# Routed attention and mixer on one core: where a pair's small TensorE products stand, and which PSUM buffers they use

## The chip, the cores and the metric

The kernel runs on one core of one Trainium2 chip. A core has several engines that work at the same time and wait for each other by semaphores: TensorE (PE in the profile) multiplies matrices and writes into PSUM, VectorE (DVE) and ScalarE (ACT) read PSUM and SBUF, GpSimd (POOL) works in SBUF, and DMA queues move data to and from the device memory. The metric is the device time of one execution in microseconds (us). Before the change it is 914.13 us, the median of three runs that lie between 913.77 and 915.92.

## The reference

Attention comes first: 4 batches, 8 heads, 768 positions, 64 channels a head. Every query and every key is assigned to the nearest of 16 cluster centres of its head, and a query sees only the keys of its own cluster. The result is joined over the heads and goes through a mixer over positions and then over channels.

```python
q_assign = argmax(einsum('bhsd,hcd->bhsc', q_n, c_n), axis=-1)     # normalised q, k, centroids
k_assign = argmax(einsum('bhsd,hcd->bhsc', k_n, c_n), axis=-1)
mask = q_assign[:, :, :, None] == k_assign[:, :, None, :]
scores = where(mask, q @ k.T / sqrt(D), -1e9)
attn = exp(scores - scores.max(-1)); attn = attn / (attn.sum(-1) + 1e-9)
x = (attn @ v) with heads joined                                    # (4, 768, 512)
h = relu(x.T @ w_tok1) @ w_tok2;  u = x + h.T                       # 768 -> 256 -> 768
out = u + relu(u @ w_ch1) @ w_ch2                                   # 512 -> 1536 -> 512
```

## The kernel before

The attention works on pairs of heads: 4 batches times 4 pairs are 16 pairs. A pair takes 4 steps (GROUPS), which are two halves of the queries (384 each) times two groups of three key chunks (NG = 3, 128 keys each). Scores are held with keys on the partitions, so that the sums over keys are made in two stages: adds on VectorE over the chunks, and a product with ones on TensorE over the partitions.

The mask is a product too. The one-hot cluster of each key, times 2^33 and less 2^33, multiplied with the one-hot cluster of each query gives 0 where the clusters agree and -2^33 elsewhere. It opens the accumulation in PSUM, and the f32 scores are added onto it.

The PSUM buffers while the attention runs: one of one bank for small products (`ps_w`), one for the sum over values (`ps_av`), and three of two banks for scores (`ps_sc`).

```python
    ps_w = pool("ps_w", 1, space=PSUM)
    ps_av = pool("ps_av", 1, space=PSUM)
    ps_sc = pool("ps_sc", NG, ps_sc_stack, space=PSUM)
    ...
    work = pool("work", 7, attention)           # the exponentials of one chunk each
```

One step's scores, sums and values:

```python
    def scores(m):
        ...
        scs = [ps_sc.tile([P, 2, 512], F32, tag="sc", name="sc") for _ in range(NG)]
        for src, start in ((st["ohT"], True), (st["T"], False)):      # masks, then q and k
            for i in range(NG):
                for h in range(2):
                    rows = slice(h * D, (h + 1) * D)
                    nc.tensor.matmul(
                        scs[i][:, h, 0:HS], lhsT=src[rows, 1, j0 + i], rhs=src[rows, 0, js],
                        start=start, stop=not start,
                    )
        for i in range(NG):
            ex = work.tile([P, 2, HS], F32, name="ex")
            nc.scalar.activation(out=ex, in_=scs[i][:, :, 0:HS], func=ACT.Exp, scale=SM_SCALE)

    def add_up(m):      # VectorE: the exponentials of the group are added into "sum"
    def values(m):      # TensorE: av += v.T @ ex; after the half's last group ScalarE copies av to avT
```

The small products of a pair:

```python
    def wtile(g, shape, dt, name):          # ps_sc for the first pair, ps_w for the others
    def turn(g):                            # VectorE: q and k of the next pair turned into "qkT"
    def route_products(g):
        pr = wtile(g, [P, a1 - a0, NJ, QP], F32, "pr")        # 4 matmuls, qkT with centroids
    def route(g):                           # VectorE: sim <- pr turned, mx = max, oh = (sim >= mx)
    def route_turn(g, a):                   # a = 1 keys, a = 0 queries
        po = wtile(g, [P, NJ, P], BF16, "po")
        for j in range(NJ):
            nc.tensor.transpose(out=po[:, j], in_=oh[:, a, j], identity=identb)
        if a == 0:
            # first pair: nc.vector.tensor_copy, the others:
            nc.scalar.copy(out=st["ohT"][:, 0], in_=po)
        else:
            nc.scalar.activation(out=st["ohT"][:, 1], in_=po, func=ACT.Copy, scale=BIG, bias=-BIG, ...)

    def half_sums(hi):                      # 4 matmuls: den = ones.T @ sum, of one half
        den = st["den"] = ps_w.tile([P, 2 * HJ, QP], F32, tag="w", name="den")
    def half_reciprocals(hi):               # VectorE: dent <- den turned, rcps = 1 / dent
    def half_turn(hi):                      # 3 transposes: px <- avT
        px = st["px"] = ps_w.tile([P, HJ, P], F32, tag="w", name="px")
    def half_out(hi):                       # VectorE: x = px * rcps
```

And the loop that gives the order, which is kept on each engine (m is the step over all pairs, s the step within a pair, g the pair):

```python
    for m in range(last + 3):
        g, s = divmod(m, GROUPS)
        more = g < NPAIR - 1
        if half_at(m - 3) is not None:
            half_out(half_at(m - 3))
        if more and s == 0:
            turn(g + 1)
        if more and s == 1:
            route(g + 1)
        if 1 <= m <= last:
            add_up(m - 1)
        if m < last:
            scores(m)
        ...
        if half_at(m - 2) is not None:                  # for s == 1 and s == 3
            half_sums(half_at(m - 2))
            half_reciprocals(half_at(m - 2))
        if more and s == 2:
            route_turn(g + 1, 1)
        if 1 <= m <= last:
            values(m - 1)
        if half_at(m - 2) is not None:
            half_turn(half_at(m - 2))
        if more and s == 0:
            route_products(g + 1)
        if more and s == 2:
            route_turn(g + 1, 0)
        ...     # loads; on every third step one piece of the mixer's weights is prepared,
                # by ScalarE (wh, wup), VectorE (wh, wh, wT) and GpSimd (wc)
```

After the loop comes the mixer (`ph`, `pu`, and then the channel part), which the change leaves as it is.

Of the kernel before, what the change touches and what calls it, by code (L numbers as in the profile page):

```python
# [18 lines left out]
P = 128  # L19
# [14 lines left out]
NG = 3  # L34
# [13 lines left out]
def kernel(  # L48
# [35 lines left out]
    def pool(name, bufs, stack=None, **kw):  # L84
        return (stack or fast).enter_context(
            tc.tile_pool(name=name, bufs=bufs, reuse_waits="tile", **kw)
        )
# [13 lines left out]
    loads = pool("loads", 3, attention)  # L101
    small = pool("small", 2, attention)
    qktp = pool("qktp", 2, attention)
    work = pool("work", 7, attention)
    sums = pool("sums", 2, attention)

    routing = fast.enter_context(ExitStack())
    qkpool = pool("qkpool", 2, routing, side="right")
    rsmall = pool("rsmall", 2, routing, side="right")
    pools = {}  # L110


# [3 lines left out]
    cnT = const.tile([P, H * C], F32, name="cnT")  # L116
    cnd = const.tile([P, NF, 2, C], F32, name="cnd")
    ohs = [rsmall.tile([P, 2, NJ, P], BF16, name=f"oh{i}", bufs=1) for i in range(2)]
    rcps = const.tile([P, 2 * NPAIR, 2, HJ], F32, name="rcps")
    cells = const.tile([P, NPAIR], F32, name="cells")  # L120

    W = {
# [55 lines left out]
    def weight_steps(pool, W, names):  # L178
# [6 lines left out]


        def tmp(name, dt, n):
            return pool.tile([P, WMAX], dt, tag=name, name=name)[:, 0:n]

        def load_bits(src, p):  # L190
            n = p["n"] = src.shape[1]
# [96 lines left out]
                in_=st["qk"][:, a].rearrange("p j i d -> p (j i d)"),  # L288
            )

    def wtile(g, shape, dt, name):

        if g == 0:
            return ps_sc.tile(shape, dt, tag="sc", name=name)
        return ps_w.tile(shape, dt, tag="w", name=name)

    def route_products(g, a0=0, a1=2):

        st, f = state[g], g % NF
        pr = wtile(g, [P, a1 - a0, NJ, QP], F32, "pr")  # L300
        for i in range(NQ):
            rows = slice(i * QP, (i + 1) * QP)
            nc.tensor.matmul(  # L303
                pr[rows], lhsT=cnd[:, f].rearrange("p i c -> p (i c)"),
                rhs=st["T"][:, a0:a1, :, rows].rearrange("p a j r -> p (a j) r"),
                start=True, stop=True,
            )
        st["pr"] = pr

    def route(g, a0=0, a1=2):  # L310

        st = state[g]
        NR = (a1 - a0) * NJ * 2
        sc = rsmall.tile([P, NR, C], F32, name="sim")
        nc.vector.transpose(
            out=sc.rearrange("p n c -> p (n c)"), in_=st.pop("pr").rearrange("p a j r -> p (a j r)")
        )
        mx = rsmall.tile([P, NR], F32, name="mx")  # L320
        nc.vector.reduce_max(out=mx, in_=sc, axis=AX.X)
        oh = ohs[g % 2][:, a0:a1].rearrange("p a j (h x) -> p (a j) h x", h=2)[:, :, :, 0:C]
        nc.vector.tensor_tensor(
            out=oh, in0=sc.rearrange("p (n h) c -> p n h c", h=2),
            in1=mx.rearrange("p (n h) -> p n h", h=2).unsqueeze(3).to_broadcast([P, NR // 2, 2, C]),
            op=ALU.is_ge,
        )

    def route_turn(g, a):

        st, oh = state[g], ohs[g % 2]
        if a == 1:
            st["ohT"] = qktp.tile([P, 2, NJ, P], BF16, name="ohT")
        po = wtile(g, [P, NJ, P], BF16, "po")
        for j in range(NJ):  # L340
            nc.tensor.transpose(out=po[:, j], in_=oh[:, a, j], identity=identb)  # L341
        if a == 0:
            if g == 0:
                nc.vector.tensor_copy(out=st["ohT"][:, 0], in_=po)  # L344
            else:
                nc.scalar.copy(out=st["ohT"][:, 0], in_=po)
        else:
            nc.scalar.activation(
                out=st["ohT"][:, 1], in_=po, func=ACT.Copy, scale=BIG, bias=-BIG,
                accum_out=cells[:, g : g + 1],  # L350
            )
# [7 lines left out]
    def scores(m):  # L359
        g, qh, j0 = split(m)  # L360
        st = state[g]
        js = slice(HJ * qh, HJ * qh + HJ)
        scs = [ps_sc.tile([P, 2, 512], F32, tag="sc", name="sc") for _ in range(NG)]
        for src, start in ((st["ohT"], True), (st["T"], False)):
            for i in range(NG):
                for h in range(2):
                    rows = slice(h * D, (h + 1) * D)
                    nc.tensor.matmul(  # L368
                        scs[i][:, h, 0:HS], lhsT=src[rows, 1, j0 + i], rhs=src[rows, 0, js],
                        start=start, stop=not start,  # L370
                    )
        for i in range(NG):
            ex = work.tile([P, 2, HS], F32, name="ex")
            nc.scalar.activation(out=ex, in_=scs[i][:, :, 0:HS], func=ACT.Exp, scale=SM_SCALE)  # L374
            st["ex", qh, j0 + i] = ex

    def add_up(m):
        g, qh, j0 = split(m)
        st = state[g]
        e = [st["ex", qh, j0 + i] for i in range(NG)]  # L380
        if j0 == 0:
            acc = st["sum", qh] = sums.tile([P, 2, HS], F32, name="sum")
            nc.vector.tensor_tensor(out=acc, in0=e[0], in1=e[1], op=ALU.add)
            e = e[2:]
        acc = st["sum", qh]
        for ex in e:
            nc.vector.tensor_tensor(out=acc, in0=acc, in1=ex, op=ALU.add)  # L387

    def values(m):
# [9 lines left out]
                    start=(j == 0), stop=(j == NJ - 1),  # L399
                )  # L400
        if j0 == NJ - NG:
            st["avT", qh] = sums.tile([P, HJ, P], F32, name="avT")
            nc.scalar.copy(out=st["avT", qh].rearrange("p j t -> p (j t)"), in_=st.pop("av"))

    def half_sums(hi):

        g, qh = divmod(hi, 2)
        st = state[g]
        acc = st.pop(("sum", qh)).rearrange("p h (j t) -> p (h j) t", j=HJ)
        den = st["den"] = ps_w.tile([P, 2 * HJ, QP], F32, tag="w", name="den")  # L410
        for i in range(NQ):
            rows = slice(i * QP, (i + 1) * QP)
            nc.tensor.matmul(den[rows], lhsT=ones, rhs=acc[:, :, rows], start=True, stop=True)  # L413

    def half_reciprocals(hi):
        g, qh = divmod(hi, 2)
        dt = small.tile([P, 2 * HJ, QP], F32, name="dent")
        nc.vector.transpose(
            out=dt.rearrange("p n r -> p (n r)"),
            in_=state[g].pop("den").rearrange("p n r -> p (n r)"),  # L420
        )
        nc.vector.reciprocal(
            out=rcps[:, hi].rearrange("p h j -> p (h j)"), in_=dt[:, :, 0]
        )

    def half_turn(hi):
        g, qh = divmod(hi, 2)
        st = state[g]
        avT = st.pop(("avT", qh))
        px = st["px"] = ps_w.tile([P, HJ, P], F32, tag="w", name="px")  # L430
        for i in range(HJ):
            nc.tensor.transpose(out=px[:, i], in_=avT[:, i], identity=ident)  # L432

    def half_out(hi):

        g, qh = divmod(hi, 2)
        b, f = divmod(g, NF)
        nc.vector.tensor_tensor(  # L438
            out=xs[b][:, HJ * qh : HJ * qh + HJ, f * P : (f + 1) * P].rearrange(
                "p j (h d) -> p j h d", h=2  # L440
            ),
            in0=state[g].pop("px").rearrange("p j (h d) -> p j h d", h=2),
            in1=rcps[:, hi].rearrange("p h j -> p j h").unsqueeze(3).to_broadcast([P, HJ, 2, D]),
            op=ALU.mult,
        )
        if qh == 1:
# [224 lines left out]
    def fits():  # L671

        inside = const.tile([P, 3, 2 * NPAIR * 2 * HJ], F32, name="inside")
        good = const.tile([P, 3], F32, name="good")
        flat = rcps.rearrange("p n h j -> p (n h j)")
        for i, (limit, op) in enumerate(((LIMIT, ALU.is_le), (1.0 / LIMIT, ALU.is_ge))):
            nc.vector.tensor_scalar(
                out=inside[:, i], in0=flat, scalar1=limit, scalar2=None, op0=op
# [22 lines left out]
    def begin():  # L701
# [27 lines left out]
        route_products(0, 0, 1)  # L729
        keep_warm(2)  # L730
        route_turn(0, 1)
        route(0, 0, 1)
        keep_warm(1)
        route_turn(0, 0)

    begin()
    weights = list(weight_steps(stage, W, ("tok1", "tok2", "ch1")))
    last = NPAIR * GROUPS
    HALF = GROUPS // 2
    ends = [lambda t=t: tok1(0, t) for t in range(NT)]  # L740
    for b in range(B):
        if b + 1 < B:
            ends += [lambda b=b, t=t: tok1(b + 1, t) for t in range(NT)]
        ends += [lambda b=b, j=j: tok2(b, j) for j in range(NJ)]

    def half_at(m):

        return m // HALF if 0 <= m < last and m % HALF == HALF - 1 else None

    for m in range(last + 3):  # L750
        g, s = divmod(m, GROUPS)
        more = g < NPAIR - 1
        if half_at(m - 3) is not None:
            half_out(half_at(m - 3))
        if more and s == 0:
            turn(g + 1)
        if more and s == 1:
            route(g + 1)
        if 1 <= m <= last:
            add_up(m - 1)  # L760
        if m < last:
            scores(m)
        if m == last:
            ps_sc_stack.close()
            pools["ps_m"] = pool("ps_m", 2, space=PSUM)
        if half_at(m - 2) is not None:
            half_sums(half_at(m - 2))
            half_reciprocals(half_at(m - 2))
        if more and s == 2:
            route_turn(g + 1, 1)  # L770
        if 1 <= m <= last:
            values(m - 1)
        if half_at(m - 2) is not None:
            half_turn(half_at(m - 2))
        if more and s == 0:
            route_products(g + 1)
        if more and s == 2:
            route_turn(g + 1, 0)
        if s == 1 and g + 2 < NPAIR:
            load(g + 2)  # L780
        if m == last - GROUPS:
# [254 lines left out]
```

## Time and profile before

| | before |
|---|---|
| time, median of 3 | 914.13 us (913.77 to 915.92) |
| span of the profiled execution | 914.3 us |
| granted TensorE clock, mean | 0.994 |
| TensorE busy | 895.6 us |
| VectorE busy | 507.3 us |
| ScalarE busy | 303.5 us |
| first score product of the first pair starts | 15.78 us |
| first score product of the last pair starts | 345.07 us |

In a line of the timeline stand the start, the time from the first start to the last end, the engine, the line of the program, the operation, what it writes and reads, the shape, and how many. An f32 product has two rows in the profile for each matmul of the program, a bf16 product one. `64*128` in front of a shape tells how many rows and columns of the array the product uses. Two products that use different rows or columns of the array run beside each other, as the two heads' scores do. The ends of matmuls are modelled; so the time that a group takes is better read from its start to the next group's start. A bracket at the end of a line gives how long the engine stood idle before it, and what ended that.

### The profile page before, as it was taken

How to read it: one execution, taken by the hardware profiler on the slowest of the kernel's cores; microseconds unless marked ns; L12 is line 12 of the kernel's file. 1: busy time of each engine (PE TensorE's matmuls, PEld its weight loads, DVE VectorE, ACT ScalarE, POOL GpSimd, SP SyncE). 2: the span in 40 equal slices, each digit the busy share in tenths (PEclk: the TensorE clock that was granted, in tenths of full speed). 3: DMA queues.
4: the chain of work that ended last, by engine and by line, in shares of the span. 5: the costliest groups of instructions: out<-in, count | busy, mean ns of one | idle time of the engine just before them, and what ended most of it. 6: DMA issues, size and time to landing. Idle time of an engine off the chain costs nothing.

```text
span 914.3 us, 11630 instructions
## 1 busy us (share of the span) xinstructions
PE 895.6 (98%) x4594; PEld 533.6 (58%) x4594; DVE 507.3 (55%) x851; ACT 303.5 (33%) x515; POOL 45.0 (5%) x40
## 2 busy tenths in 40 slices
PE   7999999999999999999999899999999999999997
PEld 3444444444444444444458568677686876858676
DVE  5787787787787875577463244333443334433342
ACT  2655565565565654231130121211212012130210
POOL 1000010010010100131000000000000000000000
PEclk9999999999999999999999899999999999999999
DMA  9725426325334100240000001000010000100001
GB/s 154 157 54 107 82 70 109 80 75 99 76 85 89 62 27 1 65 143 1 0 1 1 0 1 47 23 1 1 0 47 24 0 1 12 47 12 1 1 12 61
DMA packets 112830, 41.76 MB, mean 46 GB/s; under 512 B 101632, under 2 KB 105728, under 8 KB 112768
## 3 DMA queue, kind: packets, MB, share of 16 engines
q1 hardware_dynamic: 109632, 40.55, 19.4%
q10 hardware_dynamic: 3136, 0.39, 0.4%
q8 instruction: 38, 0.62, 0.3%
q14 instruction: 24, 0.20, 0.1%
HBM read 34.64 MB, written 6.29 MB: 45 GB/s over the span
## 4 chain that ended last, share of the span: by engine, by line
PE 92%; DVE 5%; DMA 1%; issue 1%; ACT 0%; DVEq 0%
PE sc L368 16%; PE pX L652 14%; PE pX L601 14%; PE av L397 13%; PE pZ L652 7%; PE pZ L601 7%; PE ph L470 5%; PE pu L479 5%; PE pY L652 3%; PE pY L601 3%; PE px L432 2%; DVE sum L387 2%; PE po L341 2%; PE den L413 1%; PE pr L303 1%; PE pt L542 1%
## 5 line engine op out<-in xcount | busy, mean ns | idle before, releaser
L374 ACT ACTIVATE ex<-sc 128x768 f32<-128x768 f32 x192 | 141.8, 812 | 117.5 <-PE sc L368 117.5
L397 PE MATMUL av<-ex,va 128*64 128x384 f32 x768 | 138.0, 494 | 0.0
L387 DVE TENSOR_TENSOR sum<-sum,ex 128x768 f32<-128x768 f32 x128 | 130.1, 1016 | 10.1
L368 PE MATMUL sc<-qkT 64*128 64x384 f32 x768 | 134.3, 482 | 0.0
L368 PEld LDWEIGHTS sc<-qkT 64*128 64x128 f32 x768 | 71.4, 187 | 38.0
L397 PEld LDWEIGHTS av<-ex,va 128*64 128x64 f32 x768 | 49.4, 136 | 66.2 <-issue 59.8
L601 PE MATMUL pX<-uT,wc 128*128 128x384 f32 x192 | 68.8, 495 | 1.6 <-issue 1.6
L609 ACT COPY p<-pX 128x384 f32<-128x384 f32 x24 | 11.4, 475 | 153.1 <-PE pX L601 153.1
L601 PEld LDWEIGHTS pX<-uT,wc 128*128 128x128 f32 x192 | 36.7, 193 | 26.7 <-issue 3.3
L223 POOL TENSOR_TENSOR wc<-wT,wup 128x512 int32<-128x512 int32 x24 | 32.4, 1349 | 251.2 <-DVE wT L216 251.2
L368 PE MATMUL sc<-ohT 64*128 64x384 bf16 x384 | 42.6, 327 | 0.6 <-DVE ohT L344 0.6
L479 PE MATMUL pu<-h,wt 128*128 128x512 f32 x96 | 42.0, 592 | 0.0
L470 PE MATMUL ph<-x,wt 128*128 128x512 f32 x96 | 42.0, 593 | 0.0
L496 DVE TENSOR_TENSOR x<-pX,x 128x256 f32<-128x256 f32 x24 | 10.2, 424 | 55.1 <-PE pX L652 55.1
L496 DVE TENSOR_TENSOR c<-pZ,u 128x384 f32<-128x384 f32 x24 | 13.4, 557 | 46.8 <-PE pZ L601 46.8
L652 PE MATMUL pX<-w2s,hA 128*128 128x256 f32 x144 | 36.4, 390 | 0.5 <-DVE x L496 0.5
L438 DVE TENSOR_TENSOR x<-px,rcps 128x384 f32<-128x384 f32 x32 | 17.8, 556 | 33.5 <-PE px L432 33.5
L496 DVE TENSOR_TENSOR hA<-pY,p 128x384 f32<-128x384 f32 x24 | 13.4, 557 | 40.4 <-PE pY L601 40.4
L652 PE MATMUL pX<-wc,hA 128*128 128x256 f32 x144 | 35.0, 379 | 0.0
L601 PE MATMUL pZ<-uTs,w1s 128*128 128x384 f32 x96 | 35.0, 487 | 0.0
L652 PE MATMUL pX<-w2s,hS 128*128 128x256 f32 x144 | 35.0, 379 | 0.0
L652 PE MATMUL pZ<-wc,hS 128*128 128x256 f32 x144 | 35.0, 379 | 0.0
(115 smaller groups left out, 1227.0 us busy)
## 6 DMA issues: line engine op xcount, KB each, us to landing
raw<-in_moe_w_ch_dram SPq DMA_DIRECT2D x24, 512.0 KB, 3.9
qk<-in_k_dram SPq DMA_DIRECT2D x64, 96.0 KB, 4.4
va<-in_v_dram SPq DMA_DIRECT2D x16, 384.0 KB, 3.3
out_dram<-x SPq DMA_DIRECT2D x24, 256.0 KB, 2.0
qk<-in_q_dram SPq DMA_DIRECT2D x60, 96.0 KB, 3.6
raw<-in_moe_w_tok_dram SPq DMA_DIRECT2D x3, 512.0 KB, 5.8
raw<-in_moe_w_tok_dram SPq DMA_DIRECT2D x4, 384.0 KB, 4.2
qk<-in_q_dram ACTq DMA_DIRECT2D x4, 96.0 KB, 4.8
```

The source lines that it names most:

```text
L223: nc.gpsimd.tensor_tensor(out=dst.bitcast(I32), in0=T, in1=up, op=ALU.add)
L341: nc.tensor.transpose(out=po[:, j], in_=oh[:, a, j], identity=identb)
L368: nc.tensor.matmul(scs[i][:, h, 0:HS], lhsT=src[rows, 1, j0 + i], rhs=src[rows, 0, js], start=start, stop=not start,)
L374: nc.scalar.activation(out=ex, in_=scs[i][:, :, 0:HS], func=ACT.Exp, scale=SM_SCALE)
L387: nc.vector.tensor_tensor(out=acc, in0=acc, in1=ex, op=ALU.add)
L397: nc.tensor.matmul(st["av"][h * D : (h + 1) * D], lhsT=st["va"][:, h, j], rhs=ex[:, h], start=(j == 0), stop=(j == NJ - 1),)
L432: nc.tensor.transpose(out=px[:, i], in_=avT[:, i], identity=ident)
L470: nc.tensor.matmul(pf, lhsT=W["tok1"][:, j, t * P : (t + 1) * P], rhs=xs[b][:, j], start=(j == 0), stop=(j == NJ - 1),)
L479: nc.tensor.matmul(pu, lhsT=W["tok2"][:, t, j], rhs=h1s[b][:, t], start=(t == 0), stop=(t == NT - 1))
L496: nc.vector.tensor_tensor(out=dst, in0=a, in1=b, op=ALU.add)
L601: nc.tensor.matmul(psum, lhsT=A[a][:, k, c * P : (c + 1) * P], rhs=R[r][:, k], start=start and k == 0, stop=k == 1, skip_group_check=not s ...
L652: nc.tensor.matmul(psum, lhsT=h2[a][:, k, i * P : (i + 1) * P], rhs=Bw[w][:, 3 * part + k], start=start and k == 0, stop=k == 2, skip_grou ...
```

## The change

The small products of a pair move to three places. In step 1, after the values, the denominators of the pair before (both halves at once) and the routing products of the pair after are made next to each other. In step 2, after the values, all twelve cluster transposes stand next to each other, ahead of their two copies, and the output transposes of the pair before's first half follow. In step 3 those of its second half stand alone. The denominators and routing products share one of the three score buffers, each with a bank of its own, and so do the two sets of cluster transposes; `ps_w` is left to the output transposes.

As a score buffer that a small product has used comes back later, and is then the third of the next step, the masks of the third chunk are moved behind the scores of the first two. The copy of the queries' clusters goes from ScalarE to VectorE for every pair. `sum` and `avT` hold both halves of a pair; to make room, the exponentials have six buffers in place of seven, and some other temporaries one in place of two.

```diff
-    work = pool("work", 7, attention)
+    work = pool("work", 6, attention)
-    rsmall = pool("rsmall", 2, routing, side="right")
+    rsmall = pool("rsmall", 1, routing, side="right")
...
+            bufs = 1 if name == "wT" else 2
...
-        for src, start in ((st["ohT"], True), (st["T"], False)):
-            for i in range(NG):
-                for h in range(2):
+        for chunks in (range(NG - 1), (NG - 1,)):
+            for src, start in ((st["ohT"], True), (st["T"], False)):
+                for i in chunks:
+                    for h in range(2):
...
+    def route_copy(g, a):
         if a == 0:
-            if g == 0:
-                nc.vector.tensor_copy(out=st["ohT"][:, 0], in_=po)
-            else:
-                nc.scalar.copy(out=st["ohT"][:, 0], in_=po)
+            nc.vector.tensor_copy(out=st["ohT"][:, 0], in_=po)
...
+    def pair_denominators(g):
+        dt = state[g]["dt"] = small.tile([P, 4 * HJ, QP], F32, name="dent", bufs=1)
+        nc.vector.transpose(out=dt.rearrange("p n r -> p (n r)"), in_=state[g].pop("den"))
+
+    def pair_reciprocals(g):
         nc.vector.reciprocal(
+            out=rcps[:, g].rearrange("p i h j -> p (i h j)"), in_=state[g].pop("dt")[:, :, 0]
         )
...
     for m in range(last + 3):
         g, s = divmod(m, GROUPS)
         more = g < NPAIR - 1
-        if half_at(m - 3) is not None:
-            half_out(half_at(m - 3))
+        old = g - 1 if m < last else -1
+        if s == 2:
+            if old >= 0:
+                pair_denominators(old)
+            if more:
+                route(g + 1)
+            if old >= 0:
+                pair_reciprocals(old)
+        if s == 3 and old >= 0:
+            half_out(old, 0)
+        if s == 0 and old >= 1:
+            half_out(old - 1, 1)
         if more and s == 0:
             turn(g + 1)
-        if more and s == 1:
-            route(g + 1)
         if 1 <= m <= last:
             add_up(m - 1)
         if m < last:
             scores(m)
+        if 1 <= m <= last:
+            values(m - 1)
+        if m < last and s == 1:
+            two = ps_sc.tile([P, 2, 512], F32, tag="sc", name="small")
+            if old >= 0:
+                pair_sums(old, two[:, 0, 0:HS])
+            if more:
+                route_products(g + 1, pr=two[:, 1, 0:HS])
+        if m < last and s == 2:
+            if more:
+                two = ps_sc.tile([P, 2, 1024], BF16, tag="sc", name="po")
+                for a in (1, 0):
+                    po = two[:, a, 0 : NJ * P].rearrange("p (j t) -> p j t", j=NJ)
+                    route_turn(g + 1, a, po)
+                for a in (1, 0):
+                    route_copy(g + 1, a)
+            if old >= 0:
+                half_turn(old, 0, ps_w.tile([P, HS], F32, tag="w", name="px"))
+        if m < last and s == 3 and old >= 0:
+            half_turn(old, 1, ps_w.tile([P, HS], F32, tag="w", name="px"))
...     # the lines of half_sums, route_turn, values, half_turn and route_products that stood here are gone
+        if m == last + 1:
+            pair_sums(NPAIR - 1, ps_w.tile([P, HS], F32, tag="w", name="den"))
+            pair_denominators(NPAIR - 1)
+            pair_reciprocals(NPAIR - 1)
+            half_turn(NPAIR - 1, 0, ps_w.tile([P, HS], F32, tag="w", name="px"))
+            half_turn(NPAIR - 1, 1, ps_av.tile([P, HS], F32, name="av"))
```

## The prediction

> **What bounds the kernel now.** I read part 1 of the page first, then its chain, then the attention part in order of time, because the change touches only that part.
>
> ```profile
> PE 895.6 (98%) x4594; PEld 533.6 (58%) x4594; DVE 507.3 (55%) x851; ACT 303.5 (33%) x515; POOL 45.0 (5%) x40
> PE 92%; DVE 5%; DMA 1%; issue 1%; ACT 0%; DVEq 0%
> ```
>
> TensorE (PE) is busy 98% of the span, and the chain that ended last runs through it for 92%. So a microsecond counts only if TensorE does less, pauses less between products, or waits less. A share of 98% does not say that it streams all the time: the pauses are inside it. They show in the timeline of TensorE over one pair of heads (start, length, then the product):
>
> ```profile
> 206.28 0.66 PE L368 MATMUL sc<-ohT 64*128 64x384 bf16 x6
> 206.77 2.10 PE L368 MATMUL sc<-qkT 64*128 64x384 f32 x12
> 208.80 0.53 PE L413 MATMUL den<-sum,ones 128*32 128x192 f32 x8
> 209.26 2.16 PE L397 MATMUL av<-ex,va 128*64 128x384 f32 x12
> 211.35 0.55 PE L432 MATMUL px<-ident,avT 128*128 128x128 f32 x3
> 211.83 0.66 PE L368 MATMUL sc<-ohT 64*128 64x384 bf16 x6
> ...
> 216.44 0.85 PE L303 MATMUL pr<-qkT,cnd 128*32 128x384 f32 x8
> 217.23 0.66 PE L368 MATMUL sc<-ohT 64*128 64x384 bf16 x6
> ...
> 222.91 0.55 PE L432 MATMUL px<-ident,avT 128*128 128x128 f32 x3 [0.54 <-DVE dent L418]
> ...
> 225.92 0.51 PE L341 MATMUL po<-identb,oh 128*128 128x128 bf16 x6
> 226.36 2.16 PE L397 MATMUL av<-ex,va 128*64 128x384 f32 x12
> ```
>
> I take start to next start as a block's cost: scores 2.52 us (206.28 to 208.80), values 2.09 (209.26 to 211.35), denominators den 0.46, output transposes px 0.48, routing products pr 0.79, cluster transposes po 0.44. A pair has four score and four value blocks, two each of po, den and px, and one pr: 4 x 4.61 + 2 x 1.38 + 0.79 = 21.99. The table by stretches says 22.00 for undisturbed pairs and 22.61 for the pair with the wait on 222.91:
>
> ```profile
> 200.78:223.39 22.61, 22.07 (x164) 10.16 (x164) 17.48 (x25) 12.53 (x19) 2.54 (x2) 1.00 0.54 111
> 234.44:256.44 22.00, 22.00 (x163) 10.15 (x162) 17.14 (x24) 12.40 (x19) 3.01 (x2) 1.00 0.41 78
> ```
>
> (Columns: length, then busy time of PE, PEld, DVE, ACT, POOL.) DVE works 17.1 to 17.5 us of such a pair: not the bound, but the nearest to it.
>
> Now the pause. den streams two rows of 192 columns, pr two rows of 384, in the same shape of the array. If a block is a fixed toll plus its streaming s, 0.46 = toll + s and 0.79 = toll + 2s: s = 0.33, toll = 0.13. For po: a bf16 score row of 384 columns passes in 0.16 (three in 0.49), so 128 columns take 0.054, six take 0.32, and 0.12 is left over. So **every change of block costs some 0.12 us in which nothing streams**, and a pair of 22 us has 15 blocks (8 large, 7 small).
>
> The wait at 222.91: px needs the one small PSUM buffer that den holds until DVE has turned it, and DVE is late:
>
> ```profile
> 214.16 3.04 DVE L387 TENSOR_TENSOR sum<-sum,ex 128x768 f32<-128x768 f32 x3
> 217.12 0.42 DVE L206 TENSOR_SCALAR wh<-wh 128x512 f32<-128x512 f32 x1
> ...
> 218.10 0.69 DVE L216 SCALAR_TENSOR_TENSOR wT<-raw,wh 128x512 uint32<-128x512 uint32 x1
> 218.72 0.57 DVE L317 STREAM_TRANSPOSE sim<-pr 128x384 f32<-128x384 f32 x1
> ...
> 222.48 0.37 DVE L418 STREAM_TRANSPOSE dent<-den 128x192 f32<-128x192 f32 x1
> ```
>
> A weight piece (0.42 + 0.43 + 0.69, wh to wT) stands ahead of the routing and the sums, so dent starts at 222.48 although den began at 219.75. This happened in three of the pairs.
>
> **What the skill says.** (1) The Trainium skill, "TensorEngine Tiling (Array Packing)", section Key Properties: changing the tiling mode, not just the tile, drains TensorE. The trace agrees: the blocks have modes 64\*128, 128\*64, 128\*32 and 128\*128, and the toll of 0.12 to 0.13 stands at each change, while bf16 masks to f32 scores, both 64\*128, pass without one (206.28 to 206.77 is three steps of 0.16). (2) "TensorE: Matmul & The Clock Gate", section The mechanism: matmuls start and end in program order. Agrees: at 222.91 ready scores stood behind the waiting px. So a score chunk whose buffer isn't free should stand as late as it can. (3) "SBUF — State Buffer", section Who interferes with whom: a DVE instruction with two SBUF inputs contends with GpSimd reads. Agrees: one add to sum takes 958 ns in the middle and up to 1849 ns. I take up to 0.9 us of such delay per weight piece below.
>
> **The change, part by part.**
> *Gathering.* Den of both halves (2s) and pr (2s) become one 128\*32 block: 4 x 0.33 + 0.13 = 1.45, before 2 x 0.46 + 0.79 = 1.71. Twelve po and the first px become one 128\*128 block: 0.64 + 0.36 + 0.12 = 1.12, before 2 x 0.44 + 0.48 = 1.36. The second px stays, 0.48. Seven small blocks become three, so four tolls fall away (a pair has 11 blocks in place of 15). Sum 3.05 in place of 3.55: **0.50 less per pair, 21.5**. A full gathered pair exists 14 times: 7.0 us.
> *Waits taken away.* den and pr leave the single small buffer, so px waits only for the multiply of the pair before. The 14 pairs from 35.01 to 345.07 took 310.06, or 22.15 each against 22.00: 2.1 us waiting, gone.
> *First pair and tail.* The first pair has no den and px of its own any more, 0.94, and one toll less: -1.05. The last pair gets one den of 0.79 in place of 0.46 + 0.46, one of them at the tail, and px follows den through the single buffer there as before: 1.23 from den to px now, of it the relu at 0.69 and dent at 0.37. With dent twice as wide (0.58, as the sim turn) that is some 0.5 more. With the den and px handed on from the first pair: +0.65. Together -0.4.
> *Third chunk behind two.* Per step the order is masks and scores of two chunks, then masks and scores of the third: one more change f32 to bf16 and back, inside mode 64\*128. bf16 to f32 is free; f32 to bf16 occurs nowhere in this trace. I choose 0.01 us, 64 times: +0.6.
> *DVE and ACT.* The copy of ohT's query half moves from ACT (0.80) to DVE (0.56, from its single case before). One dent of 0.58 replaces two of 0.38, one reciprocal two of 0.19: DVE +0.2 net, 17.5 of 21.5. Off the path.
> Sum: -7.0 - 2.1 - 0.4 + 0.6 = -8.9, from 914.1 to **905.2, say 905**. The mixer part after the attention keeps its instructions.
>
> **Rivals.**
> *A: the score slots become the wait.* den/pr and po now take one of the three score slots, which returns as the next step's third chunk. From the last-but-one step's start, den/pr begin at 4.6 and end near 5.9; DVE turns pr from 6.1 to 6.7. The next step begins at 6.0 and needs the slot 1.6 later, at 7.6. DVE's own queue: turn and sums of step 0 end 5.6 after its start, or 7.3 with a weight piece, so 2.7 into step 1; two adds (2.0) and 0.9 of GpSimd contention reach 5.6, dent 6.2, sim 6.8. Free by 7.0: no wait, with 0.6 to spare. After po: ACT's copy (0.83 + 0.22) ends some 1.2 after po, the slot is needed 0.5 (px) + 1.6 after: 0.8 to spare. If I am wrong by 0.5 in every pair, +7: 912. Where only weight pairs slip by 0.5: 907.
> *B: the f32 to bf16 change costs a toll.* 64 x 0.1 = 6.4: 911. Against: the mode stays the same.
> *C: DVE becomes the bound.* It would need 21.5 a pair and has 17.5. Against.
> *D: six exp buffers in place of seven.* exp of a step then waits for the sums of two steps back. The worst DVE lag above, 2.7 us, still ends the first add in time; a slip of 0.2 on ACT doesn't reach TensorE. Time as predicted.
> *E: the merged blocks pay less.* If po to px has no pause at all for the f32 weights, 0.06 a pair more: 904.
>
> **Range and chances.** A alone at its mild size and B at a third give 907 to 909; E and a smaller tail 903. So 902.5 to 910. Faster by 2% needs 895.8, more than twice the tolls and waits that I can find; slower by 2% needs a wait of 1.7 us per pair. Chances 0.02, 0.96, 0.02.
>
> **What would show it.** In the changed profile: pairs of 21.5 from score start to score start; den and pr as one block of about 1.4, po with px of about 1.1; score blocks still 2.52 (2.6 or more: B); no wait of px on dent but the last; no wait of sc on dent, sim or the ohT copy (some: A); DVE about 17.5 a pair. The mixer from its first ph on should keep its length to 1 us. Wrong would be the sum if the toll were a matter of each shape and not of the change of mode: then den and pr together would keep 1.7.

## The result, and the profile after

| | before | after |
|---|---|---|
| time, median of 6 | 914.87 us (913.77 to 915.92) | 904.85 us (903.71 to 906.34) |
| span of the profiled execution | 914.3 us | 904.5 us |
| 14 pairs of heads, from the second to the fifteenth | 310.06 us | 300.63 us |

The ratio is 0.9891, with a 95% interval of 0.9876 to 0.9905: about 10 us less. The prediction was 905.0 us with a range of 902.5 to 910.

Part 1 of the page after, and its chain:

```profile
PE 887.6 (98%) x4466; PEld 530.5 (59%) x4466; DVE 506.6 (56%) x834; ACT 295.8 (33%) x500; POOL 44.7 (5%) x40
PE 97%; DMA 1%; DVE 1%; ACT 0%; issue 0%
```

TensorE's share is the same 98%, and it is still the bound. Its busy time fell by 8.0 us, because the pauses between blocks count as busy here. VectorE, which stood in the chain with 5%, is at 1%: no wait on it is left in the pairs.

The timeline of TensorE over steps 1 and 2 of a pair after the change:

```profile
213.16 2.16 PE L400 MATMUL av<-ex,va 128*64 128x384 f32 x12
215.25 0.85 PE L417 MATMUL small<-sum,ones 128*32 128x384 f32 x8
215.91 0.83 PE L299 MATMUL small<-qkT,cnd 128*32 128x384 f32 x8
216.68 0.50 PE L369 MATMUL sc<-ohT 64*128 64x384 bf16 x4
217.01 1.45 PE L369 MATMUL sc<-qkT 64*128 64x384 f32 x8
218.30 0.33 PE L369 MATMUL sc<-ohT 64*128 64x384 bf16 x2
218.46 0.81 PE L369 MATMUL sc<-qkT 64*128 64x384 f32 x4
219.20 2.16 PE L400 MATMUL av<-ex,va 128*64 128x384 f32 x12
221.29 0.84 PE L338 MATMUL po<-identb,oh 128*128 128x128 bf16 x12
221.97 0.50 PE L430 MATMUL px<-ident,avT 128*128 128x128 f32 x3
222.40 0.50 PE L369 MATMUL sc<-ohT 64*128 64x384 bf16 x4
```

Read start to start: den with pr takes 1.43 (215.25 to 216.68), po with px 1.11 (221.29 to 222.40). The score block is still 2.52 (216.68 to 219.20) although its masks are now in two places: f32 to bf16 at 218.30 comes 1.29 after 217.01, which is four rows of 0.32, without a pause. The stretches show a single pair, and then 14 pairs together (columns: length, the busy time of PE, PEld, DVE, ACT, POOL, then granted clock, DMA share and GB/s):

```profile
205.93:227.40 21.47, 21.47 (x156) 9.96 (x154) 18.40 (x26) 13.07 (x20) 1.86 (x1) 1.00 0.39 80
34.23:334.86 300.63, 300.63 (x2159) 139.38 (x2158) 238.76 (x334) 169.87 (x258) 25.45 (x19) 1.00 0.39 81
```

300.63 / 14 = 21.47: every pair takes the same time, and TensorE's busy time equals the length of the stretch. The rest of the difference is small: the first pair gained 0.75 (18.47 in place of 19.22), the stretch from the last pair's first score to the last pair's px and the next `ph` lost 0.54 (40.20 in place of 39.66). From there to the end the two kernels take 529.5 and 529.4.

### The profile page after: what moved, and what is told of

Same layout as the page of the kernel before. It is cut to its first block, busy times and chain, and to the rows that moved or that the text cites. A ratio compares the mean times of both kernels' runs of the same rounds, so it can differ in the third digit from the quotient of the medians.

```text
span 904.5 us, 11304 instructions
## 1 busy us (share of the span) xinstructions
PE 887.6 (98%) x4466; PEld 530.5 (59%) x4466; DVE 506.6 (56%) x834; ACT 295.8 (33%) x500; POOL 44.7 (5%) x40
## 4 chain that ended last, share of the span: by engine, by line
PE 97%; DMA 1%; DVE 1%; ACT 0%; issue 0%
PE sc L369 18%; PE av L400 15%; PE pX L652 14%; PE pX L601 14%; PE pZ L652 7%; PE pZ L601 7%; PE ph L470 5%; PE pu L479 5%; PE pY L652 3%; PE pY L601 3%; PE po L338 1%; PE px L430 1%; PE small L417 1%; PE pt L542 1%; PE small L299 1%; DMA qk<-in_k_dram 1%
## 5 line engine op out<-in xcount | busy, mean ns | idle before, releaser
L375 ACT ACTIVATE ex<-sc 128x768 f32<-128x768 f32 x192 | 144.4, 811 | 102.7 <-PE sc L369 57.9
L369 PE MATMUL sc<-qkT 64*128 64x384 f32 x768 | 144.9, 483 | 0.0
L390 DVE TENSOR_TENSOR sum<-sum,ex 128x768 f32<-128x768 f32 x128 | 124.4, 972 | 9.8 <-DVE sum L390 0.9
L369 PE MATMUL sc<-ohT 64*128 64x384 bf16 x384 | 53.3, 328 | 0.7 <-DVE ohT L345 0.7
L386 DVE TENSOR_TENSOR sum<-ex 128x768 f32<-128x768 f32 x32 | 34.7, 1083 | 1.5 <-ACT ex L375 1.5
L652 PE MATMUL pZ<-w2s,hS 128*128 128x256 f32 x144 | 35.0, 379 | 0.0
L652 PE MATMUL pY<-wc,hA 128*128 128x256 f32 x144 | 35.0, 379 | 0.0
```

Of the source, the lines that this page charges most:

```text
L369: nc.tensor.matmul(scs[i][:, h, 0:HS], lhsT=src[rows, 1, j0 + i], rhs=src[rows, 0, js], start=start, stop=not start,)
L652: nc.tensor.matmul(psum, lhsT=h2[a][:, k, i * P : (i + 1) * P], rhs=Bw[w][:, 3 * part + k], start=start and k == 0, stop=k == 2, skip_grou ...
```

## The experiments

Each ratio is to the kernel before, run beside it on the same chip (median 915.63 us for experiments 1 and 3 to 5, 915.30 for 2, 7, 8 and the first of 6, 915.12 for the second of 6 and for 9). For a comparison with the changed kernel take its 0.9891. "Pair" is the time from a pair's first score to the next one's, in the trace.

**1. The masks of all three chunks first again.**

```diff
-        for chunks in (range(NG - 1), (NG - 1,)):
+        for chunks in (range(NG),):
```

> The changed kernel with the masks of all three chunks ahead of the scores again. Theory (the late third chunk is what keeps the shared score buffers from becoming a wait): in the changed kernel's trace VectorE gives the buffer of den and pr back 1.19 us after the next step's start, and that of po 1.26 us after it; the third mask would want it 0.33 us after. With some 0.2 us for the signal, two waits of about 1.0 and 1.1 us in each of 14 pairs, in all +25 to +30 us: about 932 us, more than the kernel before. Rival (the order of the chunks doesn't matter, the gain is the gathering alone): 905 us.

Measured: 934.98 us, ratio 1.0206 (1.0189 to 1.0224). A pair takes 23.38 in place of 21.47. The timeline of TensorE shows the two waits:

```profile
211.74 0.50 PE L369 MATMUL sc<-ohT 64*128 64x384 bf16 x4
212.98 0.34 PE L369 MATMUL sc<-ohT 64*128 64x384 bf16 x2 [0.74 <-DVE sim L313]
...
218.38 0.50 PE L369 MATMUL sc<-ohT 64*128 64x384 bf16 x4
219.69 0.34 PE L369 MATMUL sc<-ohT 64*128 64x384 bf16 x2 [0.81 <-DVE ohT L345]
```

The third mask would follow 0.33 after the block's start and comes 1.24 and 1.31 after it (the bracket is less than the pause, because the modelled end of the products before reaches into it). As products start in order, the f32 scores of the first two chunks, whose buffers were free, stand behind it. The gathering without this order is slower than the kernel before.

**2. The order alone, in the kernel before.** The same loop over `chunks` as in the change, and nothing else.

> The kernel before with only the third chunk's masks moved behind two chunks' scores. Theory (the order is of use only together with the shared buffers, and f32 to bf16 within one mode is free): the same as before, 914 to 915 us, score blocks 2.52. Rival (each f32 to bf16 change costs a toll of 0.1): +6.4 us, 921. Rival (the order itself brings part of the gain): under 912.

Measured: 914.75 us, ratio 1.0000 (0.9991 to 1.0009). The pairs are those of before, with the same three longer ones of 22.61, and a score block is 2.52. So the order costs nothing and brings nothing by itself; it pays only where a chunk's buffer comes late.

**3. Two blocks split off again.**

```diff
-        if 1 <= m <= last:
-            values(m - 1)
         if m < last and s == 1:
             two = ps_sc.tile([P, 2, 512], F32, tag="sc", name="small")
             if old >= 0:
                 pair_sums(old, two[:, 0, 0:HS])
+        if m < last and s == 2 and old >= 0:
+            half_turn(old, 0, ps_w.tile([P, HS], F32, tag="w", name="px"))
+        if 1 <= m <= last:
+            values(m - 1)
+        if m < last and s == 1:
             if more:
                 route_products(g + 1, pr=two[:, 1, 0:HS])
...
-            if old >= 0:
-                half_turn(old, 0, ps_w.tile([P, HS], F32, tag="w", name="px"))
```

> The changed kernel with two small blocks split off again: den between the scores and values of step 1 with pr after the values, and the first px between the scores and values of step 2 with po after the values. The same products, buffers and copies. Theory (a toll of 0.12 to 0.13 us per block): two more blocks in each of 14 pairs, 14 x 0.26 = +3.6 us: 908.5 us; a gathered pair of 21.47 becomes 21.75. Rival (gain is the small buffer's wait alone): 905 us, pair 21.47.

Measured: 909.31 us, ratio 0.9931 (0.9914 to 0.9948). Pair 21.79, which is 0.32 more for two blocks, 0.16 each, and no new wait of TensorE appears. From its timeline:

```profile
214.85 0.85 PE L417 MATMUL small<-sum,ones 128*32 128x384 f32 x8
215.64 2.16 PE L400 MATMUL av<-ex,va 128*64 128x384 f32 x12
217.72 0.85 PE L299 MATMUL small<-qkT,cnd 128*32 128x384 f32 x8
218.51 0.50 PE L369 MATMUL sc<-ohT 64*128 64x384 bf16 x4
```

den and pr take 0.79 each, 1.58 in place of 1.43 side by side.

**4. Small transposes among the values: changes of mode added.**

```diff
-            half_turn(old, 1, ps_w.tile([P, HS], F32, tag="w", name="px"))
...
     def values(m, between=None):
         for j in range(j0, j0 + NG):
             ...                           # the chunk's two products
+            if between:
+                between(j - j0)           # one px transpose of the pair before
```

> The changed kernel with the second half's three px transposes one by one after each of the three value chunks of step 3: two more px blocks and two more value blocks in a pair, each a change between the modes 128*64 and 128*128. Theory (each change of mode costs the toll of about 0.12 us or a little more): 4 x 0.12 to 0.15 = 0.5 to 0.6 per pair, 15 pairs: +7.5 to +9, 913 us. Rival (the pause belongs to the products, not to the change): 905 us.

Measured: 914.7 us, ratio 0.9991 (0.9983 to 0.9999), 9 us more than the changed kernel. Pair 22.07 to 22.13, mostly 22.08: 0.61 more for four changes, 0.15 each, and no new wait of TensorE. Nothing is computed that wasn't before, and the whole gain is spent:

```profile
206.53 0.87 PE L400 MATMUL av<-ex,va 128*64 128x384 f32 x4
207.32 0.33 PE L774 MATMUL px<-ident,avT 128*128 128x128 f32 x1
207.58 0.87 PE L400 MATMUL av<-ex,va 128*64 128x384 f32 x4
208.38 0.33 PE L774 MATMUL px<-ident,avT 128*128 128x128 f32 x1
208.63 0.87 PE L400 MATMUL av<-ex,va 128*64 128x384 f32 x4
```

A chunk of values takes 0.79 (206.53 to 207.32) and one transpose 0.25 to 0.26. Undivided, the values took 2.09 and the three transposes 0.48.

**5. One px among the po: changes of kind within a mode.** The first px transpose of the three stands between the keys' six po and the queries' six.

```diff
                 for a in (1, 0):
                     ...
                     route_turn(g + 1, a, po)
+                    if old >= 0:
+                        half_turn(old, 0, px, (0,) if a == 1 else (1, 2))
...
```

> The changed kernel with the first of the px transposes (f32) put between the keys' and the queries' six po transposes (bf16): two more changes of the kind of product in a pair, both within the mode 128*128. Theory (the toll is for the mode alone): at most 0.02 us per pair, 905 us; po ends 0.1 us later, which may leave the third chunk of the next step a wait of up to 0.1 us, then 906. Rival (every change of kind, of type or of source costs the toll): 2 x 0.12 x 14 = +3.4, 908 us.

Measured: 904.14 us, ratio 0.9876 (0.9857 to 0.9896), not to be told from the changed kernel. Pair 21.48, so 0.01 for two changes of type, source and destination:

```profile
220.02 0.51 PE L338 MATMUL po<-identb,oh 128*128 128x128 bf16 x6
220.36 0.28 PE L430 MATMUL px<-ident,avT 128*128 128x128 f32 x1
220.48 0.50 PE L338 MATMUL po<-identb,oh 128*128 128x128 bf16 x6
220.81 0.39 PE L430 MATMUL px<-ident,avT 128*128 128x128 f32 x2
```

The f32 transpose costs 0.12 here (220.36 to 220.48), hardly more than the 0.11 at which f32 transposes follow each other inside one block (220.19 to 220.52 in experiment 8, three of them), and 0.25 among the values. With experiment 4 this parts the two explanations: the toll belongs to the change of mode.

**6. The wait on dent alone, in the kernel before.** First with all weight pieces of a pair's first step moved to its second:

```diff
+    due = 0
...
-            n = m % WEVERY == 0 or m == 1
+            due += m % WEVERY == 0 or m == 1
+            n = due if s > 0 else 0
+            due -= n
```

> The kernel before with the weight pieces that are due in a pair's first step prepared in its second. Theory (px waits on dent because a weight piece stands ahead of it on VectorE): the waits of 0.6 us in four pairs go, -2.1 to -2.4 us: 912.5 us, all pairs 22.00. Rival (VectorE is late anyway): same as before, the waits come in other pairs.

Measured: 915.58 us, ratio 1.0010 (1.0001 to 1.0019): a miss. In the trace the later pairs are all 22.01, as expected, but the first took 21.8 us in place of 19.2. Its start ran at a granted clock of 0.62 (14.57 to 19.84 us), and its first step took 1.7 longer than in the kernel before. Later the cluster transposes waited 0.8 on ScalarE's copy, which stood behind the piece moved there; the kernel before has no such wait. (The expectation counted four waits of 0.6. In the trace of before three pairs are longer by 0.6 and another by 0.17; the other wait is the last pair's own, which stays.) So again, with the first pair's pieces left where they were (`s > 0 or m == 0`):

> The kernel before with the weight pieces that are due in a pair's first step prepared in its second, but the first pair's left where they were: in the run that moved all of them the waits of the later pairs were gone, every pair 22.01, and the first pair took 21.8 us in place of 19.2, with a wait of TensorE on the clusters' copy. Theory (px waits on dent because a weight piece stands ahead of it): three waits of 0.6 and one of 0.2 less and the first pair at 19.2, -2.0 us: ratio 0.9978. Rival (a piece that is moved delays something else by as much): ratio 1.000.

Measured: 913.1 us, ratio 0.9984 (0.9976 to 0.9993), and of TensorE's waits from 14 us to the mixer only those at the start and the end of the attention remain. In the kernel before the line of px was

```profile
PE px L432 <- DVE dent L418: 2.3, 4, 0.7
```

and here there are

```profile
PE px L432 <- DVE dent L418: 0.7, 1, 0.7
PE sc L368 <- DVE ohT L344: 0.6, 1, 0.6
```

(Columns: us in all, times, the longest.) All pairs from the second on take 22.01, so the 14 pairs are 2.0 us shorter; the ratio of the timed runs gives 1.5 us, with an interval of 0.6 to 2.2. That is a fifth of the gain or a little less, and could be had without the change. How much of the first try's loss the low clock made in the timed runs stays open.

**7. The queries' copy on ScalarE again.**

```diff
-            nc.vector.tensor_copy(out=st["ohT"][:, 0], in_=po)
+            if g == 0:
+                nc.vector.tensor_copy(out=st["ohT"][:, 0], in_=po)
+            else:
+                nc.scalar.copy(out=st["ohT"][:, 0], in_=po)
```

> The changed kernel with the queries' cluster copy on ScalarE again, as before the change. In the changed kernel the copy on VectorE starts only when ScalarE's copy with its sum has ended and takes 0.56 us; on ScalarE it would take 0.80, so the buffer comes free some 0.3 us later, and the third chunk of step 3 has 0.2 to 0.4 to spare. Theory: a wait of 0 to 0.15 us in 14 pairs: 905 to 907 us. Rival (ScalarE falls behind with the exponentials and TensorE waits for score buffers): 910 or more.

Measured: 904.78 us, ratio 0.9893 (0.9877 to 0.9910), pair 21.47: no difference. This part of the change neither gains nor loses. The expectation had the buffer come free 0.3 us later. It is 0.10 (1.36 us after the next score block's start in place of 1.26), because ScalarE's second copy starts right behind its first, and 0.27 is left before the third chunk's masks.

**8. One block less.** The second half's px follows the first half's directly, in the buffer of av.

```diff
-        if s == 3 and old >= 0:
-            half_out(old, 0)
-        if s == 0 and old >= 1:
-            half_out(old - 1, 1)
...
                 half_turn(old, 0, ps_w.tile([P, HS], F32, tag="w", name="px"))
+                half_turn(old, 1, ps_av.tile([P, HS], F32, name="av"))
+                half_out(old, 0)
+                half_out(old, 1)
-        if m < last and s == 3 and old >= 0:
-            half_turn(old, 1, ps_w.tile([P, HS], F32, tag="w", name="px"))
```

> The changed kernel with one block less: the second half's px directly behind the first half's in step 2, into the buffer of av, which ScalarE has emptied by then, and both multiplies right behind the copies on VectorE. Theory (toll): the px block of 0.48 becomes 0.33, 15 x 0.15 = -2.2 us: 902.7 us, pair 21.32. Rival (the multiplies give av back too late, and the values of step 3 wait): VectorE ends them about as the values start, up to +0.5 us per pair: 905 to 910 us.

Measured: 902.93 us, ratio 0.9871 (0.9855 to 0.9888), pair 21.32 as worked out. The intervals of the two ratios overlap, but each pair in the trace is 0.15 shorter. The two px take 0.76 (220.19 to 220.95), apart 0.43 and 0.48:

```profile
220.19 0.50 PE L430 MATMUL px<-ident,avT 128*128 128x128 f32 x3
220.52 0.49 PE L430 MATMUL av<-ident,avT 128*128 128x128 f32 x3
220.95 0.50 PE L369 MATMUL sc<-ohT 64*128 64x384 bf16 x4
```

**9. Four blocks less: double steps.** The scores of two steps, then the values of both. The loop is given in short.

```diff
-        for chunks in (range(NG - 1), (NG - 1,)):
+        for chunks in ((0,), (1,), (2,)):
...
+    for d in range(2 * NPAIR):
+        g, half = divmod(d, 2); m = 2 * d; more = g < NPAIR - 1; old = g - 1
+        # half 0: turn(g + 1); half 1: dent, route(g + 1), reciprocals, both multiplies of the pair before
+        scores(m); scores(m + 1); add_up(m); add_up(m + 1)
+        # half 1: all po and their copies
+        values(m); values(m + 1)
+        # half 0: den of the pair before, pr, both px of the pair before
```

> The changed kernel in double steps: the scores of two steps one after another (chunk by chunk, masks then scores), then the values of both. In the first double step den, pr and then all six px follow the values; in the second the twelve po stand between scores and values. A pair has 7 blocks in place of 11. Theory (toll per change of mode, about 0.15 with the first row's delay): two score blocks of 4.95, two value blocks of 4.03, den with pr 1.43, px 0.81, po 0.78: 21.0 per pair in place of 21.47, 15 x 0.49 = -7.3 us: 897.5 us. Rival (six chunks through three score buffers: the exponentials don't give the buffers back in time, or the adds don't give back the six exp buffers): waits of sc on ex, and 905 us or more.

Measured: 897.56 us, ratio 0.9815 (0.9802 to 0.9827): 17 us faster than before by the ratio and 7 faster than the change. The 14 pairs, and one half of one in the timeline of TensorE:

```profile
35.14:329.09 293.95, 293.95 (x2158) 145.23 (x2157) 236.58 (x336) 173.98 (x260) 23.27 (x19) 1.00 0.38 83
```

```profile
203.07 0.34 PE L369 MATMUL sc<-ohT 64*128 64x384 bf16 x2
...
208.02 4.09 PE L400 MATMUL av<-ex,va 128*64 128x384 f32 x24
212.04 0.85 PE L417 MATMUL small<-sum,ones 128*32 128x384 f32 x8
212.71 0.83 PE L299 MATMUL small<-qkT,cnd 128*32 128x384 f32 x8
213.47 0.55 PE L430 MATMUL px<-ident,avT 128*128 128x128 f32 x3
213.85 0.49 PE L430 MATMUL av<-ident,avT 128*128 128x128 f32 x3
214.27 0.34 PE L369 MATMUL sc<-ohT 64*128 64x384 bf16 x2
```

293.95 / 14 = 21.00 a pair, with 7 blocks: some pairs take 20.95 or 20.96, the others 21.02 to 21.04. Two value blocks in one take 4.02 (208.02 to 212.04), apart 2 x 2.09: 0.16 less. Two score blocks in one take 4.95 (203.07 to 208.02), apart 2 x 2.52: 0.09 less. Of what the rival had foreseen there is one wait of 0.5 on an exponential, in the first pair, and in some pairs a score product that comes 0.06 late.

## Why the prediction was right, step by step

- *Toll per block.* Right, and shown in both directions: 15, 11, 10 and 7 blocks in a pair gave 22.00, 21.47, 21.32 and 21.00, and 13 and 15 blocks made out of the changed kernel 21.79 and 22.08. The term was 0.50 per pair and measured 0.53: den with pr saved 0.28 (1.71 to 1.43), po with px 0.25 (1.36 to 1.11). By pairs the toll is 0.12 to 0.16 a block; the prediction had 0.12 to 0.13 for all. It is not the same for every block, which the prediction did not have: a score block less saved 0.09 in experiment 9, a value block less 0.16. The pause at the change is 0.09 to 0.10 in both: from row start to row start, the last f32 row of the scores is followed after 0.42 by the values, and that of the values after 0.43 by po, in place of 0.32 within a block. What the values have on top is a longer first row, 0.37 to the next one in place of 0.32. Why the first row is longer was not tried.
- *Waits on dent gone.* Right: 310.06 less 14 x 22.00 was 2.1, and no such wait is left but the last pair's. Experiment 6 removes them alone, and its trace gains as much.
- *First pair and tail.* The sum was -0.2 and not -0.4, and it is as near as that because two errors go against each other: first pair -0.75 and not -1.05, tail +0.54 and not +0.65. The first pair's 0.3 stands in its first two score blocks, 5.56 together (15.76 to 21.32) in place of 5.29. pr stands no longer between them, and the second step's masks stop for 0.15 until an exponential of the first step has ended (18.90; they go on at 18.95). The rest is the start, which ran below full speed in both traces, and longer in this one: in experiment 5 and the second run of 6, whose first products ran faster, the first pair takes 18.03 and 18.98, 0.95 less.
- *Third chunk.* The 0.6 us set aside for f32 to bf16 was too much: it is free, the score block is 2.52 in both kernels. With the 0.4 that the tolls gave beyond their term (14 x 0.03), less the 0.2 of the first pair and the tail, it is nearly all of the difference between the -8.9 of the sum and the -9.8 of the two spans.
- *Rival A, the score buffers.* No wait from the second pair on, as said, but the reserve was mis-sized: 0.6 for den with pr and 0.8 for po were given. The timeline after the change:

```profile
216.81 0.58 DVE L421 STREAM_TRANSPOSE dent<-small 128x384 f32<-128x384 f32 x1 [1.00 <-PE small L299]
217.32 0.54 DVE L313 STREAM_TRANSPOSE sim<-small 128x384 f32<-128x384 f32 x1
...
222.17 0.81 ACT L347 ACTIVATE ohT<-po 128x768 bf16<-128x768 bf16 x1 [0.29 <-PE po L338]
...
222.88 0.19 ACT L347 ACTIVATION_READ_ACCUMULATOR ohT<-po 128x1 f32 x1
...
223.10 0.56 DVE L345 COPY ohT<-po 128x768 bf16<-128x768 bf16 x1 [0.99 <-ACT ohT L347]
...
224.03 0.33 PE L369 MATMUL sc<-ohT 64*128 64x384 bf16 x2
```

dent waits for pr too, although den was done before. In experiment 3, where den ended some 2.9 us ahead of pr, VectorE still stood idle for 1.14 us until pr had ended. And VectorE's copy starts only when ScalarE's has ended, so they don't run beside each other. That both come of sharing one buffer is the likely reason, but no run has the two parts in buffers of their own. The buffers come free at 217.86 and 223.66, and the third masks start at 218.30 and 224.03: 0.44 and 0.37 to spare, the same within 0.01 in all full pairs, with the signal's way still in it. The working took the two copies as parallel. It did not matter for the time: experiment 7, with 0.10 less to spare, did not wait either. Where the room ends was not tried.
- *Rivals B, C, D and E.* B falls by experiments 2 and 5. VectorE reached 18.4 us in a pair with two weight pieces and stayed under 21.47, so C was not met. No wait on the six exp buffers (D) showed. E did not come: po with px took 1.11 where the sum had 1.12 and E 1.06.

## What to carry to other kernels

Where TensorE is busy nearly all the time, read its timeline start to start and count the changes of array mode: each cost 0.09 to 0.16 us here, whether the block that ended was a large or a small one, and the way to fewer is to put products of one mode side by side, also large ones. Gathering holds buffers longer; look which chunk gets the late buffer, and put that chunk's products last, since one that waits holds up all behind it. Before a gain is put down to one cause, take away the others alone: up to a fifth of this one was a wait that a different place for the weight pieces removes as well.

## What had not been expected of the hardware

A transpose of 128x128 costs little within its mode: 0.057 us in bf16 (twelve in 0.68) and 0.12 in f32 among bf16 ones, yet 0.25 alone between values. And the start of an execution does not always go at full speed: six of the twelve traces show a mean granted clock of 0.50 to 0.68 from 10 to 15 us, and in the two main ones the first masks took 0.73 for three steps (15.78 to 16.51, before) and 0.60 for two (15.76 to 16.36, after), later 0.49 and 0.33. In the six traces whose first pair is ordered as in the change it took 18.02 to 18.58 us, while the pairs behind it agree to 0.01 within most traces. So the first pair's time is worth less than that of the pairs after it.
